# Moving small VectorE operations of a top-k attention and MLP kernel to other engines, converting weights earlier, and shifting attention towards the first sweep

## The chip, the cores and the metric

One core of one Trainium2 chip. The metric is the device time of one execution in microseconds (us). The engines are called as in the profile: PE (TensorE, with PEld for its weight loads), DVE (VectorE), ACT (ScalarE), POOL (GpSimd) and SP (SyncE, which here issues the DMAs).

## The reference, cut to what matters

```python
scores = scale * np.matmul(q, k.transpose(0, 1, 3, 2))      # 2 x 8 heads, 576 x 576, head size 64
kth = np.partition(scores, -32, axis=-1)[..., -32:-31]
scores = np.where(scores >= kth, scores, -1000000000.0)
attn = np.exp(scores - np.max(scores, axis=-1, keepdims=True))
attn = attn / (np.sum(attn, axis=-1, keepdims=True) + 1e-09)
x = np.matmul(attn, v)                                      # as 1152 tokens x 512

h = x @ w_in                                                # 512 -> 2048
sp = np.where(h > 20.0, h, np.log1p(np.exp(np.minimum(h, 20.0))))
y = (h * np.tanh(sp)) @ w_out                               # 2048 -> 512

out = ((y @ w_a) * (y @ w_b)) @ w_out2                      # 512 -> 1536 -> 512
```

The weights arrive as float64 (two 32-bit words each) and are turned into float32 on the chip.

## The kernel before, in words

The 1152 tokens are nine tiles of 128. **Attention** runs over steps, one for each tile and pair of heads, 36 in all. A step makes the scores on PE (`scores_`: `pq` L142, `psc` L174), copies them to `s2`, and then `largest` finds the 32 largest of each row on DVE in four rounds: for each head a MAX (L190), which gives the eight largest, and a MATCH_REPLACE (L193), which strikes them out, so 8 MAX and 6 MATCH_REPLACE a step. After the first round DVE makes the negated maxima `nm` (L195), and ACT takes the exponentials (L197). `weighted_sum_` masks and sums them on DVE (the masked sum, L211, twice a step), transposes them on PE (`pe`, L219) and multiplies by v (`px`, L226). Each round ends in a `yield`, so a step is four yields, and a tile of queries is ready 16 yields on. For the keys, `prep_k` splits k into a high and a low part (`km`, `kn`: cast on ACT, L114, subtraction at L115, on DVE for both batches).

The **MLPs** run over groups of tiles (`PLAN`): first tiles 0 and 1 together, then tile 2, then the second MLP for all three; then tiles 3 to 5 through both MLPs, then tiles 6 to 8. `gated` is the first MLP, 16 chunks of 128 hidden columns, each two weight blocks of 128 x 512. Its gate takes on ACT exp(h) (L387), on DVE the clamp to e^20 (L388), on ACT a square, a logarithm and an exponential (L389 to L391), and on DVE the gate's product (L392). `bilinear` is the second MLP, 12 chunks of three blocks. From tiles 0 to 2's second MLP on, the operands are split in two parts, and a product takes three matmuls.

I call the stretches of the program A (attention alone), G0 (the first MLP, tiles 0 and 1), G1 (tile 2), B0 (second MLP, tiles 0 to 2), G2 and B1 (tiles 3 to 5), and sweep three (tiles 6 to 8). A, G0, G1 and B0 are sweep one, G2 and B1 are sweep two.

The **weights** are converted once, by `convert_`, 68 blocks in the order of use: DMA of 512 KB into `w64` (three buffers), two ACT operations (L285, L286), a shift and mask on DVE (L287), then the exponent count is added on POOL (L290), and the sign comes in by one of two ways: ACT takes the sign (L289) and POOL multiplies by it (L291), or DVE ors the sign bit in (L293) and POOL adds (L294). `SIGN` says which blocks go which way: before, all 32 blocks of the first MLP go by ACT and POOL, and of the 36 of the second every fourth. The result is in `w` (11 buffers), is stored to DRAM as `ws`, and is also kept for its first use (`fresh`); later uses load it back as `raw` (five buffers, L315). How far ahead conversions run is set by `CONV`: its first number is how many are made in A, the second and third set how many are to be made by each chunk.

What runs beside what is set by `together`, which takes turns between attention and a group's chunks: `STEPS` says how many yields of attention go beside each group. The scheduler then sorts the instructions of each engine by priority, so an engine's order is fixed when the program is built, and each engine takes its queue in that order.

Of the kernel before, what the change touches and what calls it, by code (L numbers as in the profile page):

```python
# [9 lines left out]
F32 = mybir.dt.float32  # L10
# [3 lines left out]
AF = mybir.ActivationFunctionType  # L14
ALU = mybir.AluOpType
# [14 lines left out]

SUBS = (0, 0, 0, 0, 1, 1)

KSUB = 1

SIGN = (4, 1)

ABUF = (5, 3, 2, 1, 2, 3, 1, 2)
COPIES = (0, 0, 0, 1, 4, 2)

CONV = (5, 17, 13, 2)  # L40

STEPS = (24, 22, 18, 29, 28, 0, 5)

BUFS = (3, 11, 5, 6, 1)
NEG = -3.0e38
EXP20 = 485165195.40979


@with_exitstack
def topk_attention_mlps(ctx: ExitStack, tc: tile.TileContext, q, k, v, w, out):  # L50
# [6 lines left out]
    nc = tc.nc  # L57
# [46 lines left out]
    def prep_k(b, hp):  # L104
        ks = wp.tile([P, 2, J, D], F32, name="ks", bufs=BUFS[4])
        kr = wp.tile([R, 2, D], F32, name="kr", bufs=BUFS[4])
        for s in range(2):
            nc.sync.dma_start(ks[:, s], k[b, 2 * hp + s, 0:SM, :].rearrange("(p j) d -> p j d", j=J))
        nc.sync.dma_start(kr, k[b, 2 * hp:2 * hp + 2, SM:S, :].rearrange("h p d -> p h d"))
        km = wp.tile([P, 2, J, 2, D], F32R, name="km", bufs=BUFS[4])  # L110
        kn = wp.tile([R, 2, 2, D], F32R, name="kn", bufs=BUFS[4])
        for z, raw in ((km, ks), (kn, kr)):
            high, low = (z[..., i, :] for i in range(2))
            nc.scalar.copy(high, raw)  # L114
            (nc.gpsimd, nc.vector)[KSUB].tensor_sub(low, raw, high.bitcast(F32))  # L115
        for s in range(2):
            kk = kks[:, (b * H + 2 * hp + s) % (H + 2), :]
            pk = bank("pk")
            for j in range(J):
                nc.tensor.transpose(pk[:, j * P:(j + 1) * P], km[:, s, j].rearrange("p z d -> p (z d)").bitcast(F32),  # L120
                                    ident)
            pr = bank("pr", R)
            nc.tensor.transpose(pr, kn[:, s].rearrange("p z d -> p (z d)").bitcast(F32), ident[:R, :R])
            for src, o, n in ((pk, s * R, SM), (pr, SM * (1 - s), R)):
                nc.scalar.copy(kk[:, o:o + n], src)
            KK[b, 2 * hp + s] = kk
# [52 lines left out]
    def largest(s2):  # L179
# [6 lines left out]
        for r in range(TOPK // 8):  # L186
            got = slice(8 * r, 8 * r + 8)
            src = wk if r else s2
            for s in range(2):
                nc.vector.max(m8[:, s, got], src[:, s, :])  # L190
            if r < TOPK // 8 - 1:
                for s in range(2):
                    nc.vector.match_replace(wk[:, s, :], m8[:, s, got], src[:, s, :], NEG)  # L193
            if r == 0:
                nc.vector.tensor_scalar(nm, m8[:, :, 0], -1.0, None, op0=ALU.mult)  # L195
                for s in range(2):
                    nc.scalar.activation(e2[:, s, :], s2[:, s, :], AF.Exp, bias=nm[:, s:s + 1])  # L197
            yield
# [62 lines left out]

    order = [(z, f, i) for z, F in ((0, F1), (1, F2)) for f in range(F) for i in range(2 + z)]
    fresh, stored = {}, {}
    phase, made = [0], [0, 0, 0]

    def sub():

# [3 lines left out]
    def convert(n):  # L271
        with tc.high_priority(PRI[4]):
            convert_(n)

    def convert_(n):

        while len(stored) < min(n, len(order)):
# [14 lines left out]
            else:  # L292
                nc.vector.scalar_tensor_tensor(wi, high, -0x80000000, wi, op0=ALU.bitwise_and, op1=ALU.bitwise_or)  # L293
                nc.gpsimd.tensor_tensor(wi, wi, count, op=ALU.add)  # L294
            fresh[key] = wf
            stored[key] = dp.tile([P, U], F32, name=f"ws{len(stored)}")
            nc.sync.dma_start(stored[key], wf)

# [8 lines left out]

    def weight_(split, *key):

        convert(order.index(key) + 1)  # L310
        if key in fresh:
            raw = fresh.pop(key)
# [56 lines left out]
    def gated(block, tiles, yt, at, split, second):  # L369
# [10 lines left out]
        for f in range(F1):  # L380
# [3 lines left out]
            e = ep.tile([P, T], F32, name=f"e{T}")  # L384
            g = ep.tile([P, T], F32, name=f"m{T}")
            with tc.high_priority(PRI[2]):
                nc.scalar.activation(e, ph, AF.Exp)  # L387
                nc.vector.tensor_scalar(e, e, EXP20, None, op0=ALU.min)  # L388
                nc.scalar.activation(e, e, AF.Square, bias=1.0)  # L389
                nc.scalar.activation(e, e, AF.Ln, bias=half, scale=0.5)  # L390
                nc.scalar.activation(g, e, AF.Exp, scale=-1.0)  # L391
# [108 lines left out]
```

## Time and profile before

| | |
|---|---|
| median of 3 runs | 818.53 us (816.67 to 818.68) |
| the profiled execution | 815.02 us |
| its span, first to last instruction | 813.0 us |
| busy: PE / PEld | 686.1 us (84%) / 569.2 us (70%) |
| busy: DVE | 663.7 us (82%) |
| busy: ACT / POOL | 508.2 us (63%) / 433.8 us (53%) |
| DMA | 110.12 MB, 135 GB/s |

The shares are averages over stages with different limits. A window of the trace gives the busy time of each engine in a stretch; the groups give the mean time of one kind of instruction; the chain that ended last is followed back from the last instruction.

### The profile page before, as it was taken

Reading aid. Unit: us, or ns where it says so; the run is one execution under the profiler, and the core shown is the slowest. Engines: PE = TensorE matmul, PEld = TensorE weight load, DVE = VectorE, ACT = ScalarE, POOL = GpSimd, SP = SyncE. Lnnn points to the kernel's source line nnn. Section 1 sums busy time; section 2 is a strip of 40 time slices with the busy share of each in tenths; the row PEclk is TensorE's granted clock in tenths of the full one; section 3 lists DMA queues with packets and bytes.
Section 4 is the critical chain, followed back from the end, with each engine's and each line's share of the span. In section 5 each row is a group of like instructions: output and inputs, shape, how many; then the busy total and the mean of one; then the engine's idle time right before and its main releaser. Section 6 shows DMA issues by size and latency. Waiting matters only on the chain.

```text
span 813.0 us, 12328 instructions
## 1 busy us (share of the span) xinstructions
PE 686.1 (84%) x3988; PEld 569.2 (70%) x3988; DVE 663.7 (82%) x1335; ACT 508.2 (63%) x1135; POOL 433.8 (53%) x355
## 2 busy tenths in 40 slices
PE   4475657887648889899798899998999999989997
PEld 3354435555425667688687788887998989969996
DVE  4999999999996899999999899998984277743331
ACT  6874534888857987657667698885554355652222
POOL 4550001566657420069978766665655666665661
PEclk9966776989978999999999999999999999999999
DMA  8980100667857985216544443422233354443431
GB/s 250 325 240 10 27 1 1 167 209 194 219 159 246 343 253 157 56 63 182 166 127 135 119 128 91 120 88 65 81 105 91 96 164 130 130 117 86 135 105 39
DMA packets 70753, 110.12 MB, mean 135 GB/s; under 512 B 26529, under 2 KB 30625, under 8 KB 70689
## 3 DMA queue, kind: packets, MB, share of 16 engines
q1 hardware_dynamic: 70688, 109.34, 45.5%
q8 instruction: 31, 0.51, 0.2%
q14 instruction: 34, 0.27, 0.1%
HBM read 89.13 MB, written 20.19 MB: 134 GB/s over the span
## 4 chain that ended last, share of the span: by engine, by line
PE 40%; DVE 38%; ACT 7%; issue 6%; DMA 5%; POOL 3%; SPq 0%; ACTq 0%; DVEq 0%; POOLq 0%
PE ph L351 21%; DVE m L190 14%; DVE wk L193 11%; PE acc L358 7%; PE po L358 7%; DVE e L211 5%; DMA w<-in_w_dram 4%; DVE w L293 2%; PE px L226 2%; DVE w L287 2%; PE psc L174 1%; PE pe L219 1%; DVE e L388 1%; POOL w L291 1%; POOL w L290 1%
## 5 line engine op out<-in xcount | busy, mean ns | idle before, releaser
L325 POOL TENSOR_TENSOR whl<-raw,whl 128x512 fp32r<-128x512 f32 x128 | 168.2, 1320 | 96.1 <-ACT whl L324 58.3
L351 PE MATMUL ph<-yh,whl 128*128 128x384 f32 x576 | 160.8, 346 | 7.6 <-DVE m L416 5.6
L190 DVE MAX8 m<-wk 128x8 f32<-128x576 f32 x216 | 156.8, 747 | 0.4
L290 POOL TENSOR_TENSOR w<-w,w 128x512 int32<-128x512 int32 x41 | 55.1, 1345 | 141.1 <-DVE w L287 108.0
L351 PEld LDWEIGHTS ph<-yh,whl 128*128 128x128 f32 x576 | 107.1, 192 | 12.7 <-DVE m L416 7.2
L193 DVE MATCH_REPLACE8 wk<-m,wk 128x576 f32<-128x576 f32 x144 | 106.1, 739 | 0.0
L351 PE MATMUL ph<-yl,whl 128*128 128x384 f32 x288 | 99.1, 344 | 0.3 <-DVE yl L336 0.2
L226 PE MATMUL px<-et,v 128*64 128x128 f32 (+1 forms) x800 | 74.8, 298 | 7.9 <-ACT et L220 6.5
L219 PE MATMUL pe<-ident,e 128*128 128x128 f32 x324 | 55.3, 306 | 27.5 <-DVE e L211 21.6
L365 ACT CAST gh<-m 128x384 fp32r<-128x384 f32 x68 | 34.8, 512 | 68.2 <-DVE m L416 35.0
L325 POOL TENSOR_TENSOR whl<-w,whl 128x512 fp32r<-128x512 f32 x36 | 52.5, 1468 | 40.6 <-ACT whl L324 40.6
L366 POOL TENSOR_TENSOR gl<-m,gh 128x384 fp32r<-128x384 f32 x52 | 57.6, 1107 | 30.9 <-ACT gh L365 17.5
L226 PEld LDWEIGHTS px<-et,v 128*64 128x64 f32 x800 | 54.0, 152 | 28.4 <-ACT et L220 13.7
L351 PE MATMUL ph<-xh,whl 128*128 128x384 f32 x256 | 71.7, 340 | 0.6 <-DVE m L392 0.6
L211 DVE SCALAR_TENSOR_TENSOR e<-s,m,e 128x576 f32<-128x576 f32 x72 | 70.6, 987 | 1.1 <-ACT e L197 0.9
L219 PEld LDWEIGHTS pe<-ident,e 128*128 128x128 f32 x324 | 43.5, 157 | 35.1 <-issue 20.2
L220 ACT COPY et<-pe 128x384 f32<-128x384 f32 x108 | 49.8, 489 | 24.9 <-PE pe L219 24.1
L322 DVE CAST whl<-raw 128x512 fp32r<-128x512 f32 x59 | 42.4, 719 | 24.5 <-PE po L358 11.5
L324 ACT CAST whl<-raw 128x512 fp32r<-128x512 f32 x77 | 47.1, 621 | 24.1 <-PE ph L351 12.9
L197 ACT ACTIVATE e<-s,nm 128x576 f32<-128x576 f32 x72 | 52.3, 775 | 12.1 <-DVE nm L195 12.1
L358 PE MATMUL po<-whl,gh 128*128 128x512 f32 x216 | 58.9, 397 | 0.5 <-ACT gh L365 0.5
L174 PE MATMUL psc<-kks,qh 128*128 128x288 f32 x160 | 51.4, 342 | 9.2 <-ACT s L176 2.6
(87 smaller groups left out, 1619.9 us busy)
## 6 DMA issues: line engine op xcount, KB each, us to landing
raw<-ws SPq DMA_DIRECT2D x168, 256.0 KB, 2.7
w<-in_w_dram SPq DMA_DIRECT2D x68, 512.0 KB, 4.2
ws<-w SPq DMA_DIRECT2D x68, 256.0 KB, 4.3
qr<-in_q_dram SPq DMA_DIRECT2D x16, 256.0 KB, 4.1
ks<-in_k_dram SPq DMA_DIRECT2D x16, 128.0 KB, 4.5
v<-in_v_dram SPq DMA_DIRECT2D x16, 128.0 KB, 4.5
out_dram<-o SPq DMA_DIRECT2D x8, 256.0 KB, 2.8
qr<-in_q_dram SPq DMA_DIRECT2D x4, 128.0 KB, 4.8
```

Of the source, the lines that this page charges most:

```text
L174: nc.tensor.matmul(psc, qq[:, s, :], kk[:, a * HS:(a + 1) * HS], start=(n == 0), stop=(n == len(parts) - 1))
L190: nc.vector.max(m8[:, s, got], src[:, s, :])
L193: nc.vector.match_replace(wk[:, s, :], m8[:, s, got], src[:, s, :], NEG)
L197: nc.scalar.activation(e2[:, s, :], s2[:, s, :], AF.Exp, bias=nm[:, s:s + 1])
L211: nc.vector.scalar_tensor_tensor(e2[:, s, :], s2[:, s, :], kth[:, s:s + 1], e2[:, s, :], op0=ALU.is_ge, op1=ALU.mult, accum_out=sm[:, 2 * ...
L219: nc.tensor.transpose(pe[:, i, :], ef[:, n * P:(n + 1) * P], ident)
L226: nc.tensor.matmul(px[s * D:(s + 1) * D, o:o + n], vt[b][:, 2 * hp + s, j, :] if j < J else v4[b][:, hp, s, :], et[:, i if j < J else J, o ...
L290: nc.gpsimd.tensor_tensor(wi, wi, count, op=ALU.add)
L325: sub().tensor_sub(wl, raw, wh.bitcast(F32))
L351: nc.tensor.matmul(ph, a, x, start=(i == 0), stop=(i == len(mm) - 1))
L358: nc.tensor.matmul(acc[i], z[:, i * P:(i + 1) * P], a, start=(first and m == 0), stop=(last and m == len(mm) - 1))
L366: sub().tensor_sub(gl, g, gh.bitcast(F32))
```

## The change

```diff
-KSUB = 1
-
-SIGN = (4, 1)
+KSUB = (0, 1)
+
+SIGN = (4, 4)
...
-CONV = (5, 17, 13, 2)
-
-STEPS = (24, 22, 18, 29, 28, 0, 5)
+CONV = (26, 28, 15, 2)
+
+STEPS = (28, 25, 20, 26, 13, 0, 5)
...
-EXP20 = 485165195.40979
...
-            (nc.gpsimd, nc.vector)[KSUB].tensor_sub(low, raw, high.bitcast(F32))
+            (nc.gpsimd, nc.vector)[KSUB[b]].tensor_sub(low, raw, high.bitcast(F32))
...
-                nc.vector.tensor_scalar(nm, m8[:, :, 0], -1.0, None, op0=ALU.mult)
+                nc.scalar.mul(nm, m8[:, :, 0], -1.0)
...
-            fresh[key] = wf
+            if len(stored) < made[3] + BUFS[1] - 2:
+                fresh[key] = wf
...
+        made[3] = max(made[3], order.index(key))
         convert(order.index(key) + 1)
...
-                nc.scalar.activation(e, ph, AF.Exp)
-                nc.vector.tensor_scalar(e, e, EXP20, None, op0=ALU.min)
+                nc.vector.tensor_scalar(e, ph, 20.0, None, op0=ALU.min)
+                nc.scalar.activation(e, e, AF.Exp)
```

The key subtractions of batch 0 go to POOL. The negated maxima go to ACT. The signs of all 68 blocks go by ACT and POOL. The clamp is taken of h, by DVE from PSUM, before the exponential. A block that is converted nine or more places ahead of the block in use is not kept: it is stored, and loaded back when it is used (224 loads of `raw` in place of 168). 26 blocks are asked for in A. Attention's yields beside G0, G1 and B0 rise from 24, 22 and 18 to 28, 25 and 20.

The scheduler's order then holds these numbers of instructions in each stage, before and after. On DVE and ACT a stage begins with its first gate product (G) or bilinear product (B), on PE with its first product of the group. Line numbers are those of before.

| engine, instruction | A | G0 | G1 | B0 | G2 | B1 |
|---|---|---|---|---|---|---|
| DVE weight shift L287 | 12, 34 | 29, 34 | 8, 0 | 19, 0 | 0, 0 | 0, 0 |
| DVE sign L293 | 0, 0 | 6, 0 | 6, 0 | 15, 0 | 0, 0 | 0, 0 |
| DVE MAX L190 | 80, 82 | 48, 50 | 43, 50 | 44, 50 | 49, 48 | 24, 8 |
| DVE MATCH_REPLACE L193 | 60, 61 | 36, 39 | 32, 38 | 34, 36 | 36, 36 | 18, 6 |
| DVE masked sum L211 | 18, 20 | 12, 12 | 10, 12 | 13, 13 | 13, 13 | 6, 2 |
| DVE nm L195 | 10, 0 | 6, 0 | 6, 0 | 5, 0 | 6, 0 | 3, 0 |
| DVE key pairs L115 | 5, 1 | 0, 1 | 3, 2 | 0, 0 | 0, 0 | 0, 0 |
| PE psc L174 | 82, 82 | 46, 54 | 80, 80 | 40, 48 | 48, 48 | 24, 8 |
| PE pe L219 | 72, 72 | 45, 54 | 60, 63 | 45, 51 | 57, 51 | 45, 33 |
| PE px L226 | 80, 80 | 50, 60 | 90, 110 | 60, 50 | 70, 60 | 50, 40 |
| PE pq L142 | 22, 22 | 10, 12 | 12, 14 | 10, 10 | 14, 12 | 4, 2 |
| PE prs L240 | 16, 16 | 8, 8 | 8, 16 | 16, 8 | 8, 16 | 16, 8 |

Two places of DVE's order show what this does. The first is the middle of A. `m` is a step's list of largest scores, `s` the scores, `wk` the scores with the found ones struck out, `e` the exponentials, `ql` the low part of q. Before:

```order
L193 MATCH_REPLACE wk<-m_683,wk 128x576
L190 MAX m_760<-s_647 128x8
L193 MATCH_REPLACE wk<-m_683,wk 128x576
L193 MATCH_REPLACE wk<-m_760,s_647 128x576
L190 MAX m_683<-wk 128x8
L193 MATCH_REPLACE wk<-m_760,s_647 128x576
L195 TENSOR_SCALAR nm<-m_760 128x2
L190 MAX m_683<-wk 128x8
L153 SCALAR_TENSOR_TENSOR ql<-pq,qh 128x256
```

With the change (line numbers of the changed kernel):

```order
L189 MAX m_826<-wk 128x8
L192 MATCH_REPLACE wk<-m_936,s_768 128x576
L152 SCALAR_TENSOR_TENSOR ql<-pq,qh 128x256
L189 MAX m_826<-wk 128x8
L189 MAX m_936<-wk 128x8
L210 SCALAR_TENSOR_TENSOR e_824,sm<-s_646,m_826,e_824 128x576
L286 TENSOR_SCALAR w<-w 128x512
L189 MAX m_936<-wk 128x8
L210 SCALAR_TENSOR_TENSOR e_824,sm<-s_646,m_826,e_824 128x576
L192 MATCH_REPLACE wk<-m_936,wk 128x576 x2
L286 TENSOR_SCALAR w<-w 128x512
```

The search no longer has `nm` in it, and the weight shifts `w<-w` (now L286) stand between its pieces.

The second is the middle of B0; `m_...<-ph,e` is the bilinear product. Before:

```order
L287 TENSOR_SCALAR w<-w 128x512
L190 MAX m_4053<-wk 128x8 x2
L293 SCALAR_TENSOR_TENSOR w<-w_3897,w 128x512
L193 MATCH_REPLACE wk<-m_4053,wk 128x576
L287 TENSOR_SCALAR w<-w 128x512
L193 MATCH_REPLACE wk<-m_4053,wk 128x576
L190 MAX m_4053<-wk 128x8
L293 SCALAR_TENSOR_TENSOR w<-w_3910,w 128x512
L190 MAX m_4053<-wk 128x8
L211 SCALAR_TENSOR_TENSOR e_4051,sm<-s_3536,m_4053,e_4051 128x576
L153 SCALAR_TENSOR_TENSOR ql<-pq,qh 128x256
L416 TENSOR_TENSOR m_3709<-ph,e_3708 128x384
```

With the change:

```order
L192 MATCH_REPLACE wk<-m_4598,s_4226 128x576
L189 MAX m_4598<-wk 128x8
L192 MATCH_REPLACE wk<-m_4598,wk 128x576
L189 MAX m_4598<-wk 128x8
L189 MAX m_4598<-s_4226 128x8
L192 MATCH_REPLACE wk<-m_4598,wk 128x576
L192 MATCH_REPLACE wk<-m_4598,s_4226 128x576
L417 TENSOR_TENSOR m_4199<-ph,e_4198 128x384
L189 MAX m_4598<-wk 128x8 x2
L192 MATCH_REPLACE wk<-m_4598,wk 128x576
```

Shifts and signs are gone from this stage; between two bilinear products stands search alone.

## Rows read from the trace of the kernel before

**Rows 1.** Windows by stage: us, each engine's busy time, PE clock, DMA share, GB/s.

```profile
0.00:133.00 133.00, 76.52 (x408) 57.29 (x408) 121.90 (x269) 75.01 (x168) 31.58 (x30) 0.78 0.43 130
133.00:262.00 129.00, 94.03 (x426) 62.41 (x427) 121.62 (x244) 97.86 (x216) 78.79 (x64) 0.89 0.65 183
262.00:334.00 72.00, 63.48 (x485) 49.16 (x483) 67.15 (x162) 59.85 (x170) 17.50 (x24) 0.98 0.74 237
334.00:467.00 133.00, 118.26 (x763) 103.46 (x764) 131.31 (x246) 86.44 (x183) 100.00 (x74) 0.97 0.40 121
467.00:562.00 95.00, 91.27 (x569) 77.75 (x567) 90.77 (x191) 79.77 (x179) 60.74 (x49) 1.00 0.36 103
562.00:666.00 104.00, 103.23 (x641) 93.30 (x642) 64.40 (x121) 47.02 (x101) 63.44 (x52) 1.00 0.33 98
666.00:813.00 147.00, 139.29 (x702) 125.80 (x701) 66.55 (x107) 62.24 (x121) 81.80 (x65) 0.99 0.38 109
```

**Rows 2.** Chain that ended last, 562 to 666 us, by line.

```profile
by line: PE ph L351 54.2%; PE po L358 24.2%; PE px L226 7.8%; PE pe L219 5.3%; PE psc L174 2.8%; PE prs L240 1.6%; POOL gl L366 1.1%; issue 1.1%; PE pq L142 0.7%; DVE yl L336 0.6%; PE acc L358 0.5%; DVE whl L322 0.3%; POOL whl L325 0.2%
```

**Rows 3.** The same chain of the whole run, pieces: start, us, what.

```profile
60.04 2.65 DVE m L190 x4
75.65 1.48 DVE e L211 x4
79.84 1.46 DVE wk L193 x2
```

**Rows 4.** Groups of DVE, 0 to 133 us: busy us, mean ns | idle before.

```profile
L211 DVE SCALAR_TENSOR_TENSOR e<-s,m,e 128x576 f32<-128x576 f32 x16 | 12.6, 804 | 0.0
L287 DVE TENSOR_SCALAR w<-w 128x512 int32<-128x512 int32 x11 | 5.3, 482 | 2.1 <-ACT w L285 2.1
L115 DVE TENSOR_TENSOR km<-ks,km 128x512 fp32r<-128x512 f32 x5 | 4.5, 895 | 0.9 <-ACT km L114 0.9
L115 DVE TENSOR_TENSOR kn<-kr,kn 64x128 fp32r<-64x128 f32 x5 | 3.5, 691 | 0.3 <-ACT kn L114 0.3
L195 DVE TENSOR_SCALAR nm<-m 128x2 f32<-128x2 f32 x10 | 2.8, 284 | 0.0
```

**Rows 5.** Groups of DVE, 133 to 262 us.

```profile
L287 DVE TENSOR_SCALAR w<-w 128x512 int32<-128x512 int32 x30 | 17.7, 591 | 2.3 <-ACT w L285 2.3
L211 DVE SCALAR_TENSOR_TENSOR e<-s,m,e 128x576 f32<-128x576 f32 x14 | 15.6, 1125 | 0.0
L388 DVE TENSOR_SCALAR e<-e 128x256 f32<-128x256 f32 x16 | 12.0, 753 | 1.6 <-ACT e L387 1.6
L392 DVE SCALAR_TENSOR_TENSOR m<-m,ph 128x256 f32<-128x256 f32 x16 | 6.5, 406 | 1.7 <-ACT m L391 1.7
L293 DVE SCALAR_TENSOR_TENSOR w<-w,w 128x512 int32<-128x512 int32 x6 | 5.1, 842 | 0.1
```

**Rows 6.** Groups of DVE, 262 to 334 us.

```profile
L287 DVE TENSOR_SCALAR w<-w 128x512 int32<-128x512 int32 x8 | 4.6, 571 | 0.8 <-ACT w L285 0.7
L293 DVE SCALAR_TENSOR_TENSOR w<-w,w 128x512 int32<-128x512 int32 x6 | 4.1, 680 | 0.1
```

**Rows 7.** Groups of DVE, 334 to 467 us.

```profile
L293 DVE SCALAR_TENSOR_TENSOR w<-w,w 128x512 int32<-128x512 int32 x15 | 17.8, 1189 | 0.0
L287 DVE TENSOR_SCALAR w<-w 128x512 int32<-128x512 int32 x19 | 15.4, 811 | 0.0
```

**Rows 8.** Groups of POOL and ACT, whole run.

```profile
L291 POOL TENSOR_TENSOR w<-w,w 128x512 f32<-128x512 f32 x41 | 56.1, 1369 | 2.6
L289 ACT ACTIVATE w<-w 128x512 f32<-128x512 f32 x41 | 28.0, 682 | 0.1
```

**Rows 9.** Waits of the whole run: us in total, times, longest us.

```profile
PE acc L358 <- DVE m L392: 27.8, 14, 9.2
DVE w L287 <- ACT w L285: 5.2, 7, 1.3
```

**Rows 10.** Waits, 666 to 813 us.

```profile
ACT e L389 <- DVE e L388: 12.7, 13, 1.5
```

More of the change, by code (lines that the diff above doesn't have):

```diff
@@ L263, in topk_attention_mlps @@
     fresh, stored = {}, {}
-    phase, made = [0], [0, 0, 0]
+    phase, made = [0], [0, 0, 0, 0]
     def sub():
```

## The prediction

> **What bounds the kernel now.** I read the windows by stage first [rows 1]. They fall into two halves. From 0 to 467 us, the stages A, G0, G1 and B0, DVE is busy for 442 of 467 us, and in every one of the four it is busier than PE. From 467 us on, PE is busy for 91 of 95, 103 of 104 and 139 of 147 us. So sweep one lasts as long as DVE's queue, and what follows lasts as long as PE's work. The chain that ended last says the same of B1: 97% of it stands under PE's matmuls [rows 2]. A DVE saving therefore counts in sweep one, and a matmul moved out of sweeps two and three counts there. G2 alone is near both limits.
>
> Two readings give prices. The chain's pieces show the pace of a full DVE queue: four MAX in 2.65 us (0.66 each), two MATCH_REPLACE in 1.46 (0.73 each), two masked sums with their accumulator reads in 1.48 (0.74 each) [rows 3]. The groups, window by window, show that some DVE operations cost more the busier POOL is. POOL's share is 24% in A, 61% in G0 and 75% in B0 [rows 1]. The weight shift at L287 takes 482 ns in A, 591 in G0, 811 in B0 [rows 4, 5, 7], and the masked sum at L211 takes 804 in A and 1125 in G0 [rows 4, 5].
>
> **The change, stage by stage.** The counts are those of the table of the order; a stage's extra work on DVE is added to its length, since DVE sets it.
>
> *A.* Search and masked sums: two MAX, one MATCH_REPLACE and two sums more, 1.3 + 0.7 + 1.5 = +3.5 us. Shifts: 34 in place of the 11 of the window, at the 591 ns of G0, because POOL's share here comes near G0's (31.6 us, and 22 conversions with two operations of 1.37 [rows 8], and the key subtractions, some 98 us of about 149, or 66%): 20.1 - 5.3 = +14.8. For the same reason 20 masked sums at 1125 in place of 804 ns: +6.4. Gone from DVE: four pairs of key subtractions, 4 x (895 + 691) = -6.3, and the negated maxima, -2.8 [rows 4]. Sum **+15.6**. The ends: with 482 ns and no dearer sums it is +5.5; with 811 it is +23.1.
>
> *G0.* Search: two MAX and three MATCH_REPLACE, +3.5. Shifts: 34 for 30; POOL's share rises to about 79% (16 operations more), above B0's, but the neighbours are G0's, so I take 0.70, the middle of 591 and 811: 23.8 - 17.7 = +6.1. The six signs leave, -5.1, and seven negated maxima at A's 284 ns, -2.0. The clamp moves in front of the exponential, so its source is ph in PSUM. No row shows that form. The nearest is the gate's product at L392, also from PSUM, same shape, 406 ns, against 753 for the clamp as it stands [rows 5]: 16 x 0.347 = -5.6. One key pair of batch one comes here, +1.6. Sum **-1.5**; with 591 -5.2, with 811 +2.3.
>
> The clamp's row says that PSUM is the cheaper source here: 406 against 753 ns [rows 5]. The Trainium skill (VectorE: DVE Perf Modes, "Why PSUM operands drop a tier") says the reverse of it: an fp32 operation with one source runs at double rate from SBUF and at single rate from PSUM. By that rule alone the 16 clamps would not fall in price and the sum below would be some 6 us higher. The trace doesn't agree in this stage, since 753 ns for 256 columns is no double rate.
>
> *G1.* Seven MAX, six MATCH_REPLACE and two sums more, 4.6 + 4.4 + 1.5 = +10.5. Gone: eight shifts -4.6, six signs -4.1 [rows 6], one key pair -1.6. Sum **+0.2**.
>
> *B0.* No conversion is left: 19 shifts and 15 signs, -33.2 [rows 7]; six MAX and two MATCH_REPLACE come, +5.4. DVE alone would let the stage shrink by 27.8 of 133 us. But PE then becomes the bound. B1 has the same products and took 104 us at full PE [rows 1]. Against it, B0 has 24 score matmuls, six transposes of e and six of q more, and eight of the reciprocals' fewer. B1's shares over its counts price these at 0.121, 0.122, 0.18 and 0.104 us [rows 2]: +3.9, so 108. Some 8 us pass before the first product, hence 116: **-17**. The ends are -12, if PE doesn't keep that density, and -27.8, if PE gets the attention's part done earlier.
>
> *G2 and B1.* Two search steps have left for sweep one: 16 score matmuls, 18 transposes, 20 products with v and four transposes of q, at 0.121, 0.122, 0.162 and 0.18 us [rows 2]: 1.9 + 2.2 + 3.2 + 0.7 = **-8.0**, all on PE's path.
>
> *Sweep three.* The clamp before the exponential saves a handover between ACT and DVE. ACT waits there 12.7 us in 13 times for the clamp [rows 10], mostly behind PE; I take **-1**, between 0 and -12.7.
>
> At nothing I cost: the 27 signs and the negated maxima on ACT (0.68 us for a sign [rows 8]; with all three ACT operations of a conversion at that price, A's ACT goes from 75 to about 122 of 149 us, G0's from 98 to about 114, so both stay below DVE); the clamp's wait for ph, since PE waits 27.8 us for the gate and is ahead of DVE [rows 9], which if not so would cost DVE each lateness of PE; and 56 more reloads of 256 KB, 14 MB, in stages whose DMA share is 0.74 at most [rows 1], prefetched into five buffers. Shifts wait for ACT 5.2 us in all 68 [rows 9]; 23 more in A are worth 2 us and stand in the range.
>
> Sum: 15.6 - 1.5 + 0.2 - 17 - 8 - 1 = **-11.7 us**. The profiled execution took 815.0 us (span 813.0, 2.0 around it), so 803.3. The median of the runs is 818.5, 3.5 above it, and on that scale the forecast is 818.5 - 11.7 = 806.8, **807 us**. What a measurement of this kernel can tell from no change is about 0.3%, 2.5 us: 816 to 821 counts as the same.
>
> **The rivals.** *Better: sweep one keeps DVE's whole saving.* If the shifts in A stay at A's 482 ns and the sums at 804 (-10.1), or PE works off attention early enough in G1 that B0 shrinks by DVE's 27.8 (-10.8), the time is about 796, with both 786. For it: PE has idle time in G1 [rows 1]. Against it: POOL's share.
>
> *Slower: A and G0 are paced by POOL.* All 68 conversions are now packed into these two stages, with two POOL operations each. If POOL runs there nearly without gaps, each of the 68 shifts and 32 masked sums waits for a good part of a POOL operation. Half of one is 0.68 us [rows 8]; over the 482 and 804 of A that is 1.16 and 1.49 us, and against what I took: A 34 x 0.57 + 20 x 0.36 = 27, G0 34 x 0.46 + 12 x 0.36 = 20, together 47, or 854 us; a quarter of an operation gives about 820. It decides from 0.12 us a piece above my prices, since 100 x 0.12 is the whole gain. For it: the steps from 482 to 591 to 811. Against it: 811 at 75%, and the signs that leave DVE are such operations too. The Trainium skill (SBUF — State Buffer, "SBUF: two separate sides") states the rule behind it: POOL and those DVE operations hold one pair of ports exclusively, for a whole instruction. The rows agree in direction; they show 0.3 us at G0's share.
>
> *Nothing gained.* A at its upper end (+7.5), B0 at -12 (+5): 807 + 12.5 = 819. The freed time would lie idle on DVE in B0 and G2.
>
> **How the numbers follow.** My forecast, 798 to 816: 0.56. Better: 0.22. Nothing gained: 0.10. Slower: 0.12. The range takes in the better rival without its tail and reaches above to the quarter operation and the two waits of 2 us: 785 to 822. Faster: 0.22 + 0.51 of the 0.56 = 0.73; the same: 0.05 + 0.08 = 0.13; slower: 0.14.
>
> **What would show it.** Right: A longer by 10 to 20 us, G0 about as long, no L287 after G0, B0 near 116 us with PE over 95% busy and DVE idle there for the first time, B1 near 98. The clamp's mean at 256 columns near 406 ns. Wrong: shifts over 900 ns or masked sums over 1300 in A and G0 (POOL), B0 still full on DVE, or PE idle in B0 behind a reload or POOL's subtraction of the weight parts.

## The result, and the profile after

The changed kernel is slower, by a little: median 821.60 us of 8 runs (820.69 to 825.18) against 818.39 us of 8 runs of the kernel before (815.94 to 819.89). The ratio of the runs is 1.006, with a 95% interval of 1.0043 to 1.0076 (the two medians alone give 1.004). The forecast was 807 us, with a range of 785 to 822. The time lies just inside the range, but on the other side of no change. The profiled execution after took 821.38 us, its span 819.5 us, against 815.02 and 813.0 before. The spans thus differ by 6.5 us and the medians by 3.2, because the profiled execution before was 3.4 us faster than its median; what follows goes by spans.

DVE's busy time fell, as it was meant to: 663.7 us before, 620.4 us after. But the windows below show where the 43 us went: 36.8 of them left the last stretch, where PE sets the pace and DVE is idle for a third of the time and more, and 26.0 left B0, while A gained 7.8 and the middle 11.7. Over sweep one, which DVE bounded, its work fell by 6.5 us only. What has to be explained is why the middle got more work, and why that which left B0 and the last stretch gave so little.

For the comparison I cut both runs at the same three points of the program: the first product of G0, the first product of B0, and the first accumulation of G2. I call the second stretch, G0, G1 and the turn to B0, the **middle**. First the windows of the kernel before at these points (columns as in [rows 1]: length, then busy us of PE, PEld, DVE, ACT and POOL, PE's clock, DMA share, GB/s):

```profile
0.00:133.00 133.00, 76.52 (x408) 57.29 (x408) 121.90 (x269) 75.01 (x168) 31.58 (x30) 0.78 0.43 130
133.00:342.00 209.00, 162.30 (x969) 115.44 (x970) 196.77 (x425) 162.35 (x396) 96.29 (x87) 0.92 0.66 195
342.00:468.30 126.30, 114.77 (x712) 100.89 (x712) 123.31 (x227) 83.11 (x175) 101.30 (x75) 0.97 0.43 130
468.30:813.00 344.70, 332.48 (x1903) 295.55 (x1901) 221.72 (x416) 187.74 (x398) 204.67 (x164) 1.00 0.36 104
```

And after:

```profile
0.00:142.30 142.30, 80.00 (x409) 58.47 (x409) 129.65 (x269) 108.81 (x236) 89.70 (x76) 0.78 0.72 223
142.30:365.20 222.90, 177.97 (x1070) 126.61 (x1070) 208.51 (x447) 176.42 (x435) 114.90 (x100) 0.88 0.72 216
365.20:479.30 114.10, 111.77 (x689) 100.43 (x690) 97.30 (x195) 66.93 (x149) 63.15 (x51) 0.99 0.29 83
479.30:819.50 340.20, 328.67 (x1824) 290.64 (x1822) 184.91 (x355) 180.91 (x381) 205.93 (x164) 0.98 0.36 105
```

So A is 9.3 us longer, the middle 13.9 longer, B0 12.2 shorter, and the rest (G2 to the end) 4.5 shorter: +6.5 us in all. In B0, PE is busy for 111.8 of 114.1 us, and DVE, which had 3 us left there before, now has 17. In the middle DVE had 11.7 us more to do, although signs, negated maxima and part of the clamp had left it.

The groups of DVE say why. From 0 to 142 us (busy us, mean ns | idle before), which answers to [rows 4]:

```profile
L286 DVE TENSOR_SCALAR w<-w 128x512 int32<-128x512 int32 x30 | 17.6, 587 | 4.7 <-ACT w L284 4.7
L210 DVE SCALAR_TENSOR_TENSOR e<-s,m,e 128x576 f32<-128x576 f32 x16 | 17.3, 1092 | 0.0
```

From 142 to 282 us, which is G0 and answers to [rows 5]:

```profile
L286 DVE TENSOR_SCALAR w<-w 128x512 int32<-128x512 int32 x38 | 29.0, 764 | 2.4 <-ACT w L284 1.3 <-issue 0.8
L210 DVE SCALAR_TENSOR_TENSOR e<-s,m,e 128x576 f32<-128x576 f32 x16 | 18.4, 1159 | 0.0
L388 DVE TENSOR_SCALAR e<-ph 128x256 f32<-128x256 f32 x16 | 6.6, 411 | 1.9 <-PE ph L352 1.8
```

The shift costs 764 ns in G0, where 591 stood before. The clamp from PSUM costs 411 ns where 753 stood.

The middle ends with a turn. G1's last accumulation starts at 343.7 us, and B0's first product comes 21.5 us later; before, these were 331.2 and 342.0, 10.8 us apart. All lengths of the turn below are counted so. PE's timeline in the turn, before and after (start, us, engine, line, op, [idle before and its releaser]):

```profile
330.74 1.02 PE L358 MATMUL acc<-raw,m 128*128 128x512 f32 x2
...
339.21 0.60 PE L341 MATMUL pt<-ident,y 128*128 128x128 f32 x4
339.65 0.60 PE L219 MATMUL pe<-ident,e 128*128 128x128 f32 x4
341.83 0.44 PE L219 MATMUL pe<-ident,e 128*128 128x128 f32 x2 [1.58 <-DVE e L211]
342.02 0.72 PE L351 MATMUL ph<-yh,whl 128*128 128x384 f32 x2
```

After:

```profile
343.31 1.02 PE L359 MATMUL acc<-raw,m 128*128 128x512 f32 x2
...
348.30 1.09 PE L239 MATMUL prs<-ident,rs 128*64 128x128 f32 x16 [0.89 <-DVE rs L235]
...
353.92 0.85 PE L173 MATMUL psc<-kks,ql 128*128 128x288 f32 x2 [3.03 <-DVE ql L152]
...
359.56 2.15 PE L218 MATMUL pe<-ident,e 128*128 128x128 f32 x9 [3.84 <-DVE e L210]
361.64 1.11 PE L225 MATMUL px<-et,v 128*64 128x128 f32 x6
362.69 0.66 PE L342 MATMUL pt<-ident,y 128*128 128x128 f32 x4
...
365.18 0.62 PE L352 MATMUL ph<-yh,whl 128*128 128x384 f32 x2 [0.45 <-ACT yh L335]
```

B0's first product needs y of tile 2 transposed (`pt`). In PE's fixed queue `pt` now stands behind `pe`, the transposes of an attention step's `e`, which wait for that step's search on DVE; before, it stood in front of them. The chain of 344 to 365 us agrees: nearly all of it is search.

```profile
by line: DVE m L189 47.9%; DVE wk L192 38.8%; DVE e L210 7.0%; issue 5.3%; DVE x L241 2.8%; DVE ql L152 1.6%; DVE rs L234 0.3%; DVE rs L235 0.3%
```

DVE works through the whole turn (21.0 of the 21 us from 344 to 365). The turn is therefore not a stall of DVE; it is DVE's backlog of attention, made visible on PE.

Counted over the same four stretches, MAX and MATCH_REPLACE together are: before 132, 155, 92 and 126, after 131, 181, 95 and 98. The 28 that left the last stretch did not go to B0, where DVE now idles. They went to the middle, where DVE is busy for 208.5 of 222.9 us.

### The profile page after: what moved, and what is told of

Same layout as the page of the kernel before. It is cut to its first block, busy times and chain, and to the rows that moved or that the text cites. A ratio compares the mean times of both kernels' runs of the same rounds, so it can differ in the third digit from the quotient of the medians.

```text
span 819.5 us, 12468 instructions
## 1 busy us (share of the span) xinstructions
PE 698.4 (85%) x3988; PEld 576.2 (70%) x3988; DVE 620.4 (76%) x1264; ACT 533.1 (65%) x1198; POOL 473.7 (58%) x390
## 4 chain that ended last, share of the span: by engine, by line
PE 55%; DVE 8%; ACT 1%; issue 1%; POOL 0%; DMA 0%; ACTq 0%; POOLq 0%
PE ph L352 28%; PE po L359 9%; PE acc L359 8%; DVE m L189 4%; PE px L225 3%; DVE wk L192 3%; PE pe L218 2%; PE psc L173 2%; DVE e L210 1%; PE pq L141 1%; PE pt L342 1%; PE prs L239 1%; ACT y L400 1%; DVE m L393 0%; DMA raw<-ws 0%
## 5 line engine op out<-in xcount | busy, mean ns | idle before, releaser
L326 POOL TENSOR_TENSOR whl<-raw,whl 128x512 fp32r<-128x512 f32 x161 | 214.0, 1337 | 166.7 <-ACT whl L325 136.8
L352 PE MATMUL ph<-yh,whl 128*128 128x384 f32 x576 | 157.8, 345 | 1.5 <-ACT yh L335 1.5
L289 POOL TENSOR_TENSOR w<-w,w 128x512 int32<-128x512 int32 x68 | 89.3, 1313 | 73.0 <-DVE w L286 38.7
L325 ACT CAST whl<-raw 128x512 fp32r<-128x512 f32 x110 | 67.6, 622 | 45.5 <-PE ph L352 22.0
L290 POOL TENSOR_TENSOR w<-w,w 128x512 f32<-128x512 f32 x68 | 94.0, 1383 | 5.4 <-ACT w L288 0.7
L417 DVE TENSOR_TENSOR m<-ph,e 128x384 f32<-128x384 f32 x36 | 20.0, 555 | 88.1 <-PE ph L352 80.1
L218 PE MATMUL pe<-ident,e 128*128 128x128 f32 x324 | 56.9, 313 | 29.5 <-DVE e L210 20.1
L210 DVE SCALAR_TENSOR_TENSOR e<-s,m,e 128x576 f32<-128x576 f32 x72 | 74.8, 1048 | 1.8 <-ACT e L196 1.2
L284 ACT ACTIVATE w<-w 128x512 f32<-128x512 f32 x68 | 45.9, 675 | 31.3 <-DMA w<-in_w_dram 19.4
L189 DVE MAX8 m<-s 128x8 f32<-128x576 f32 x72 | 53.2, 748 | 15.7 <-ACT s L175 15.5
L173 PE MATMUL psc<-kks,ql 128*128 128x288 f32 x160 | 49.2, 339 | 17.6 <-DVE ql L152 17.6
```

Of the source, the lines that this page charges most:

```text
L173: nc.tensor.matmul(psc, qq[:, s, :], kk[:, a * HS:(a + 1) * HS], start=(n == 0), stop=(n == len(parts) - 1))
L210: nc.vector.scalar_tensor_tensor(e2[:, s, :], s2[:, s, :], kth[:, s:s + 1], e2[:, s, :], op0=ALU.is_ge, op1=ALU.mult, accum_out=sm[:, 2 * ...
L218: nc.tensor.transpose(pe[:, i, :], ef[:, n * P:(n + 1) * P], ident)
L290: nc.gpsimd.tensor_mul(wf, wf, highf)
L325: nc.scalar.copy(wh, raw)
L326: sub().tensor_sub(wl, raw, wh.bitcast(F32))
```

## The experiments

The change has three separable parts. I call them the **moves** (key subtractions of batch 0 and all signs off DVE, negated maxima to ACT, clamp ahead of the exponential), the **early conversions** (`CONV` and the rule for kept blocks) and the **shares** (`STEPS`). Lengths below are given for A, middle, B0, rest; those of the kernel before are 133.0, 209.0, 126.3 and 344.7 us. Times are medians, and each ratio is against the kernel before on the same chip.

### The parts alone and in pairs

**e1_engines**: the kernel before with the moves alone.

```diff
+KSUB = (0, 1)
+SIGN = (4, 4)
...
+                nc.scalar.mul(nm, m8[:, :, 0], -1.0)
...
+                nc.vector.tensor_scalar(e, ph, 20.0, None, op0=ALU.min)
+                nc.scalar.activation(e, e, AF.Exp)
```

> Before, with the four moves between engines only (key subtractions of batch 0 and all signs on POOL, negated maxima on ACT, clamp ahead of the exponential); conversions and attention's shares as before. Theory 1 (the early conversions lose the time, by making shifts dearer in A and G0 and by leaving DVE idle in B0; the moves by themselves gain): 795 to 808 us. Theory 2 (the moves lose it, because 37 us more of POOL's work blocks DVE): 819 to 830 us.

Measured 817.90 us, 1.0021 (1.0002 to 1.0039): no gain. Its windows:

```profile
0.00:129.30 129.30, 76.19 (x409) 57.26 (x409) 116.18 (x250) 76.43 (x178) 37.56 (x38) 0.80 0.45 134
129.30:339.10 209.80, 166.82 (x963) 116.86 (x963) 181.37 (x397) 172.06 (x418) 113.38 (x99) 0.92 0.65 194
339.10:475.90 136.80, 127.25 (x844) 110.39 (x845) 134.98 (x270) 105.71 (x232) 122.10 (x91) 0.98 0.42 124
475.90:816.20 340.30, 322.87 (x1775) 286.08 (x1774) 183.89 (x350) 178.73 (x371) 205.76 (x163) 0.99 0.36 103
```

In the middle DVE is busy for 181.4 us, 15.4 less than before, and the stretch is no shorter: the freed time became idle time, 28.4 us where there were 12.2. What DVE waited for in the middle (us in total, times, longest), in the kernel before:

```profile
DVE m L392 <- ACT m L391: 4.2, 5, 2.1
DVE w L287 <- ACT w L285: 3.1, 4, 1.2
```

and in e1:

```profile
DVE m L392 <- ACT m L391: 11.9, 7, 3.1
DVE w L287 <- ACT w L285: 8.2, 9, 2.5
DVE e L387 <- PE ph L351: 4.3, 6, 1.7
```

These are handovers of the gate (its product `m` waits for ACT, the clamp `e` for PE's `ph`) and of the weights (the shift waits for ACT). The order put 34 more search operations into B0 (126 for 92), where conversions still stand, so B0 grew by 10.5. Neither theory held.

**g1_convonly**: the kernel before with the early conversions alone.

```diff
-CONV = (5, 17, 13, 2)
+CONV = (26, 28, 15, 2)
...
+            if len(stored) < made[3] + BUFS[1] - 2:
```

> Before, with the early conversions and their rule only: old shares, old engines. If the early conversions gain by themselves (B0 bound by PE, some 100 us): 808 to 815 us. If they gain only beside the moves that make room on DVE in A and G0: 820 to 835 us (the kernel with the new shares too, 841, less the 10 to 13 us that the shares cost).

Measured 827.59 us, 1.0113 (1.0088 to 1.0139). A 151.8, middle 213.0, B0 113.5, rest 348.5. B0 falls by 12.8, but A pays 18.8, with DVE busy for 140 of its 152 us.

**e4_engines_conv**: moves and early conversions, that is, the changed kernel with the old shares.

```diff
-STEPS = (28, 25, 20, 26, 13, 0, 5)
+STEPS = (24, 22, 18, 29, 28, 0, 5)
```

> The changed kernel with attention's shares as before (the moves, the early conversions and the rule stay). Theory 1: 816 to 826 us, A and G0 still long. Theory 3 (the new shares of attention lose the time, by the wait between G1 and B0 that grew from 11 to 21 us): 805 to 812 us, and that wait back at 11 us.

Measured 811.09 us, 0.9934 (0.991 to 0.9958). Each of the two alone gains nothing or loses; together they gain. A takes 151.8 us in g1 and 142.0 here, so the conversions need the room that the moves make on DVE there; B0 takes 136.8 us in e1 and 112.5 here, so the moves need it free of conversions.

```profile
0.00:142.00 142.00, 80.14 (x409) 58.63 (x409) 127.36 (x269) 108.40 (x236) 89.43 (x76) 0.75 0.72 223
142.00:351.50 209.50, 171.66 (x970) 119.07 (x970) 184.37 (x407) 168.20 (x415) 112.14 (x99) 0.89 0.74 226
351.50:464.00 112.50, 112.49 (x744) 101.05 (x745) 101.77 (x204) 69.57 (x154) 66.22 (x53) 1.00 0.34 94
464.00:809.00 345.00, 331.87 (x1869) 294.75 (x1867) 200.47 (x386) 186.08 (x394) 205.08 (x163) 0.99 0.36 102
```

The middle is as long as before (209.5), although DVE has 12.4 us less to do there; no engine is full in it. DVE's waits for the gate are again the largest:

```profile
DVE m L394 <- ACT m L393: 8.3, 7, 1.8
DVE e L389 <- PE ph L353: 6.4, 8, 2.1
```

B0 is already at PE's limit (112.49 busy of 112.50) without the new shares.

**e2_schedule** (early conversions and shares, no moves), **e3_engines_steps** (moves and shares) and **h2_steps_only** (shares alone, on the kernel before) complete the set. All three have this line, e2 also g1's edit and e3 also e1's:

```diff
-STEPS = (24, 22, 18, 29, 28, 0, 5)
+STEPS = (28, 25, 20, 26, 13, 0, 5)
```

> Before, with the early conversions, the rule on what is kept and the new shares of attention only; all operations on their old engines. Theory 1: 822 to 840 us, since the 27 signs on DVE now also stand in A and G0. Theory 2: 805 to 818 us.

> The changed kernel with the conversions and the rule on what is kept as before (the moves and the new shares of attention stay). Theory 1: 795 to 808 us, shifts spread over A, G0, G1 and B0 as before. Theory 2: 819 us or more, as the changed kernel.

> Before, with the new shares of attention only. If the shares lose whatever the rest is: 826 to 832 us (10 to 13 more, as in the two pairs measured). If they lose only because of the place of the transposes, which here stand behind two thirds of a step: 818 to 825 us.

Measured: e2 840.84 us, 1.029 (1.0257 to 1.0322); e3 831.13 us, 1.0176 (1.0145 to 1.0207); h2 827.13 us, 1.0126 (1.0108 to 1.0145). The shares lose wherever they are added. By spans and stretches:

| shares added to | A | middle | B0 | rest | span |
|---|---|---|---|---|---|
| the kernel before (h2) | +1.5 | +9.2 | +0.7 | +0.2 | +11.6 |
| the moves (e1 to e3) | +1.7 | +11.7 | +2.9 | -4.3 | +12.0 |
| moves and early conversions (e4 to after) | +0.3 | +13.4 | +1.6 | -4.8 | +10.5 |

The loss is in the middle each time. What DVE did in the middle, in us:

| kernel | length | DVE busy | DVE idle |
|---|---|---|---|
| before | 209.0 | 196.8 | 12.2 |
| shares alone (h2) | 218.2 | 212.9 | 5.3 |
| moves (e1) | 209.8 | 181.4 | 28.4 |
| moves and shares (e3) | 221.5 | 199.6 | 21.9 |
| moves and early conversions (e4) | 209.5 | 184.4 | 25.1 |
| all three (after) | 222.9 | 208.5 | 14.4 |

The moves take work from DVE and give it back as idle time. The shares bring 16 to 24 us of work and lengthen the stretch by 9 to 13, since a part of it fills idle time.

### Is it the place of one step, or the amount of attention in the middle?

My first reading of the turn was that one attention step stands in front of `pt`, and that taking it out would restore the 10.8 us. **f2_g1_22** takes three yields out of G1, **f5_mid** takes G0 and G1 back to the old shares and gives B0 more; both are the changed kernel but for `STEPS`.

```diff
-STEPS = (28, 25, 20, 26, 13, 0, 5)
+STEPS = (28, 22, 23, 26, 13, 0, 5)
```

> The changed kernel with three of attention's yields moved from G1 to B0 (28, 22, 23, 26, 13): in PE's order the transposes of tile 2's y then stand in front of the transposes of one more attention step, where the changed kernel has them behind. Theory 3 (the time is lost in the wait between G1 and B0, because those transposes stand behind a step that DVE has yet to search): the wait falls from 21 to 10 to 12 us, the time to 808 to 813. Theory 1 (the early conversions lose it in A and G0, the wait only takes up what is late anyhow): 818 us or more.

Measured 814.92 us, 0.9979 (0.9953 to 1.0004). The turn is 17.6 us, not the 10 to 12 expected, and the middle 220.2: a miss. `pt` does stand a step earlier, but 174 search operations are still ahead of B0's first product. The time is 7 us below the changed kernel's, in small parts: middle and B0 some 3 us each, the rest 2.

```diff
-STEPS = (28, 25, 20, 26, 13, 0, 5)
+STEPS = (24, 22, 24, 27, 15, 0, 5)
```

> The changed kernel with attention's yields 24, 22, 24, 27, 15: A, G0 and G1 as with the old shares, and six yields more in B0, where DVE stood idle 15 of 113 us. Theory 3: the wait stays near 10 us, and the work comes out of sweep two: 804 to 810 us, at or below the kernel with the old shares (811). If B0 has no room: 812 or more.

Measured 811.12 us, 0.9929 (0.991 to 0.9949). The middle is 212.9 with 160 search operations. But more yields for B0 put no more search there (101; e4 had 103), so it gains nothing over e4. Its profiled execution took 816.03 us, the longest of its eight, so its stretches are some 5 us long in sum against the median.

**h1_same_sum** gives G0 and G1 together the 46 yields that they had before, and B0 the rest, so that sweep one has the changed kernel's 73.

```diff
-STEPS = (28, 25, 20, 26, 13, 0, 5)
+STEPS = (28, 18, 27, 26, 13, 0, 5)
```

> The changed kernel with attention's yields 28, 18, 27, 26, 13: sweep one has 73 yields as in the changed kernel, but seven of them stand behind the end of G1, so that in PE's order the transposes of tile 2's y follow the last product of G1 at once. If the loss is in those transposes' place (theory 3): the wait between G1 and B0 falls from 21 us below 8, and the time to 803 to 810 us. If sweep one merely has too much attention in it, and the wait is where that shows: 814 us or more, with the time given back in G1 or B0.

Measured 814.10 us, 0.997 (0.9955 to 0.9984). `pt` comes right behind G1's last accumulation and the turn falls to 5.3 us, as expected. The time falls by 7.5 us against the changed kernel, not by the 12 to 19 expected, since G0 and G1 take back 6 of the 16 us (207.5 for 201.4) and the rest is 3.5 us longer. This lies on the border of the two readings and does not part them: the edit moves `pt` and takes nine search operations out of the middle at once. The turn by itself is not the measure, since 16 us of it are worth 10 in the middle; the middle as a whole, 212.8 us with 172 search operations, is the thing to look at.

Over all kernels here but two, the middle goes with that count: with 154 to 160 search operations it takes 203 to 213 us (before, e1, e4, f5, and f8, g2, g5, h4 below), with 163 to 172 it takes 213 (g1, h1, and g4 below), with 174 to 181 it takes 218 to 223 (f2, h2, e3, after, and f4 below). The exceptions are g3, 219.5 us with 159, and e2, 232.0 us with 180, which has 27 signs on DVE in the middle besides. From e4 to after it is 23 operations and two masked sums for 13.4 us; at 0.735 us and 1.1 us a piece they are 19 of the 24.1 us by which DVE's work grew, and DVE's idle time fell by 10.7. The count and the place of `pt` change together in most of these kernels, so that the count is the cause is argued from DVE's work, not shown by an edit that changes it alone.

### What POOL's work costs DVE

**f4_nomul**: the changed kernel without POOL's multiplication by the sign.

```diff
-                nc.gpsimd.tensor_mul(wf, wf, highf)
```

> The changed kernel without POOL's multiplication by the sign (weights keep no sign): 68 operations, 94 us, less on POOL in A and G0. Theory 4 (POOL's work makes DVE's shifts and masked sums dearer there): shifts fall from 587 and 764 ns to below 520 in both stages, masked sums from 1092 and 1159 to below 1000, A and G0 together from 282 to 262 to 270 us. If DVE's prices have another cause: prices as they are, 278 us or more.

Measured 808.04 us, 0.9892 (0.987 to 0.9914). POOL's busy time in the middle falls from 114.9 to 57.2 us. DVE's groups from 142.9 to 282 us:

```profile
L286 DVE TENSOR_SCALAR w<-w 128x512 int32<-128x512 int32 x33 | 16.1, 489 | 3.0 <-ACT w L284 2.3 <-issue 0.6
L210 DVE SCALAR_TENSOR_TENSOR e<-s,m,e 128x576 f32<-128x576 f32 x16 | 15.6, 984 | 0.0
L387 DVE TENSOR_SCALAR e<-ph 128x256 f32<-128x256 f32 x16 | 6.6, 414 | 7.9 <-PE ph L351 7.9
```

The shift goes from 764 to 489 ns in G0 and from 587 to 413 in A, the masked sum from 1159 to 984 in G0 but only from 1092 to 1044 in A (below 1000 was expected), with nothing taken out but POOL's multiplication. The clamp, whose source is now in PSUM, does not move (411 and 414). A and G0 together end at 274 us (ACT's first copy of G0's y, at 281 in the changed kernel), between the two expectations. The time falls by 13.6 us (11.9 in the profiled executions), but not all of it by these prices: in the middle DVE has 15.9 us less to do and the stretch is 5.2 us shorter, A is 0.6 longer, and 7.3 us come from B0 and the rest, where nothing is converted. The Trainium skill (SBUF — State Buffer, "SBUF: two separate sides") has the rule that a POOL operation and a DVE operation in a two-port mode or with two inputs in SBUF hold a shared pair of ports exclusively, for the whole instruction; this run agrees with it for the shift and the sum.

**f8_signdve**: e4 with the second MLP's signs back on DVE (and the old shares).

```diff
-SIGN = (4, 4)
+SIGN = (4, 1)
```

> The changed kernel with the old shares of attention, and the signs of 27 blocks back on DVE: against the kernel with the old shares (811 us) it shows what the move of the signs is worth where conversions are early. The move pays (DVE is full there): 820 to 832 us. It doesn't, since POOL's multiplications cost DVE as much in dearer shifts: 807 to 815 us.

Measured 809.71 us, 0.9912 (0.9885 to 0.994), against e4's 811.09 and 0.9934: the move of the signs is worth nothing. In the middle 27 signs come to 20.1 us on DVE, the 38 shifts fall from 25.6 to 20.2 us because POOL has 77 in place of 112 us to do, and most of the rest goes into the 25 us in which DVE idled in e4's middle, of which 18 are left.

### The other moves, each taken back from f8

**g2_noclamp** puts the clamp behind the exponential again, **g3_nonm** the negated maxima on DVE, **g4_noksub** all key subtractions on DVE.

```diff
-                nc.vector.tensor_scalar(e, ph, 20.0, None, op0=ALU.min)
-                nc.scalar.activation(e, e, AF.Exp)
+                nc.scalar.activation(e, ph, AF.Exp)
+                nc.vector.tensor_scalar(e, e, 485165195.40979, None, op0=ALU.min)
```

> Early conversions, old shares, 27 signs on DVE (810 us), and the clamp back behind the exponential. By the rows the clamp's move saves DVE some 7 us in G0 and G1: 813 to 819 us. By the rule on PSUM sources alone it saves nothing: 807 to 812 us.

Measured 813.62 us, 0.9949 (0.9929 to 0.9968): the clamp's move is worth about 4 us, at the lower end of what was expected. Its old form cost 506 ns here, with POOL busy for 44% of G0, against 753 at 61% in [rows 1, 5].

```diff
-                nc.scalar.mul(nm, m8[:, :, 0], -1.0)
+                nc.vector.tensor_scalar(nm, m8[:, :, 0], -1.0, None, op0=ALU.mult)
```

> The same base (810 us) with the negated maxima back on DVE. By the rows they cost DVE some 6 us in A, G0 and G1: 814 to 818 us. If ACT's round trip hides them: 807 to 812 us.

Measured 826.66 us, 1.011 (1.0079 to 1.014), 17 us over f8 and far over what I expected (some 9 us above the upper end). `nm` itself is busy for 9.0 us in A and the middle, which are 5.5 and 9.7 us longer. The remaining 6 us there, and the middle that is long for its count of searches, I cannot put down to `nm`; the order changed with it. That stays open.

```diff
-KSUB = (0, 1)
+KSUB = (1, 1)
```

> Early conversions, old shares, 27 signs on DVE (810 us), and the key subtractions of batch 0 back on DVE. By the rows the move saves DVE 5 to 6 us in A: 813 to 817 us. If POOL's later subtractions cost PE and DVE as much: 807 to 811 us.

Measured 818.54 us, 1.0032 (1.001 to 1.0054), some 9 us over f8 and above what I expected. A is 4.8 us longer, the middle 3.3 and B0 4.5, the rest 5.6 shorter in the profiled execution, which at 815.3 us was faster than the median.

### A version that beats both

**g5_best** joins f5's shares with f8's signs, **h4_sum_signdve** h1's shares with f8's signs. h4 against the changed kernel:

```diff
-SIGN = (4, 4)
+SIGN = (4, 1)
...
-STEPS = (28, 25, 20, 26, 13, 0, 5)
+STEPS = (28, 18, 27, 26, 13, 0, 5)
```

> The same base (810 us) with attention's yields 24, 22, 24, 27, 15. The version meant to be the fastest: 803 to 809 us if six more yields beside B0 fill DVE's idle time there and leave sweep two; 809 to 812 if, as with the signs on POOL, the scheduler leaves B0's order as it was.

> The yields 28, 18, 27, 26, 13 and 27 signs back on DVE, all else as changed. Meant to beat both kernels: 802 to 809 us if the transposes' place was the loss and the signs on DVE cost nothing; 810 us or more if not.

Measured: g5 810.16 us, 0.9894 (0.9865 to 0.9924), no better than f8. h4 **801.36 us, 0.9816 (0.9793 to 0.984)**, the fastest here. Its windows:

```profile
0.00:143.10 143.10, 80.47 (x409) 59.12 (x409) 127.43 (x269) 109.09 (x237) 89.68 (x76) 0.77 0.72 222
143.10:346.40 203.30, 169.04 (x972) 118.61 (x972) 197.29 (x431) 155.39 (x389) 79.22 (x72) 0.91 0.73 238
346.40:462.10 115.70, 114.32 (x754) 101.80 (x752) 104.17 (x216) 69.33 (x157) 66.58 (x53) 1.00 0.30 87
462.10:798.40 336.30, 326.31 (x1860) 291.41 (x1857) 198.30 (x378) 182.56 (x391) 204.28 (x162) 0.99 0.36 103
```

Its search counts are 131, 156, 108 and 111: one more than before in the middle, 16 more in B0, 15 fewer in the last stretch. This is what the shares were thought to do. h1, with the same yields, had 172 and 92 in the middle and B0; the scheduler's order put 16 operations elsewhere once the signs were DVE's. So taking the signs back is worth 12.7 us here and nothing in f8. For the 9.5 us of it in the middle the order is the likely reason, not the signs' own price: DVE does 4.8 us less there and idles 4.7 us less. That isn't shown by an edit of the order alone. With equal search left in the last stretch, h4 is 8.4 us shorter there than the kernel before and h1 only 1.0. PE's idle time makes 4.5 of the 7.4 us between them, and its busy time 2.9. Part of both lies where G2 hands over to B1. In h1, PE waits there 4.2 us for ACT's copy of y, and then has a granted clock of 0.52, close to the lower of its two levels (1.2 GHz), for 14 us; in h4 the same place shows 0.83 over 10 us. First h1, then h4:

```profile
561.00:575.00 14.00, 9.45 (x34) 7.83 (x35) 13.26 (x29) 6.21 (x12) 0.00 (x0) 0.52 0.06 19
550.00:560.00 10.00, 7.40 (x40) 5.92 (x39) 10.00 (x21) 7.70 (x17) 2.53 (x2) 0.83 0.14 46
```

Why h1's handover takes longer I have not settled.

## Why the prediction was wrong

Against its own terms, by the three cuts:

| stretch | forecast | measured |
|---|---|---|
| A, G0, G1, up to B0's first product | +15.6 - 1.5 + 0.2 = +14.3 | +9.3 + 13.9 = +23.2 |
| B0 | -17 | -12.2 |
| G2, B1, sweep three | -8 - 1 = -9 | -4.5 |
| sum | -11.7 | +6.5 |

That the time lies inside the range is luck of opposite errors: -6.3 us in A against +15.2 in the middle, +4.8 in B0 and +4.5 behind it. By part of the change, with the prediction's own terms (the split is mine: B0's -17 counts with the conversions) and the spans:

| part | forecast | measured |
|---|---|---|
| moves and early conversions (before to e4) | -17.7 | -4.0 |
| of that, up to B0's first product, behind A | -1.3 - 14.0 = -15.3 | +0.5 |
| shares (e4 to after) | 14.0 - 8.0 = +6.0 | +10.5 |

**The step that failed is the rule "a stage's extra work on DVE is added to its length, since DVE sets it", where it credits savings to G0 and G1.** Without the search and sums that arrive there (3.5 + 10.5 = 14.0 us), the prediction has these two stages shrink by 15.3 us, for the signs, the negated maxima and the clamp, less dearer shifts. The saving itself was nearly right: e4 has 12.4 us less work on DVE in the middle. But the stretch is 0.5 us longer. In e1 it is 15.4 us less work and 0.8 us longer. The whole saving became DVE's idle time, 25.1 and 28.4 us where the kernel before has 12.2. DVE was the busiest engine there but no longer the pace: it waits at the gate's handovers. The clamp's wait for `ph`, which the prediction put at nothing "since PE waits 27.8 us for the gate and is ahead of DVE", is 6.4 us in e4, 4.3 in e1 and 3.5 after; the gate product's wait for ACT is 4.2 us before and 8.3 and 11.9 in e4 and e1. That these waits are what holds the stretch up is read from the traces; no run takes them away.

**The shares were mis-sized too**, by 4.5 us. The prediction added by stage and never set their price beside their return; by its own terms they lose 6 us, and the three pairs of runs show 10.5 to 12.0. The arrival looks right (14.0 forecast, 9.2 to 13.4 measured in the middle), but by luck: DVE's work there grew by 16.1 to 24.1 us, and idle time took up the rest. The return was 0 to 5 us in place of 8. Some of it may have gone to the clock: in the last stretch the granted clock is 1.00 before and 0.98 after, which for a full PE is at most some 7 us (an estimate: 2% of 340 us). And B0 could pay nothing back, since with the conversions gone it stands at PE's limit whether the shares are old or new (112.5 and 114.1 us).

**The counts hid a part of it.** The table of the order gave G0 and G1 18 search operations more and B0 8. In the trace the middle has 26 more and B0 3, so search costs DVE some 6 us more in the middle than was summed. The order's stage on an engine ends where that engine reaches the next stage's instruction, and in the turn DVE's search runs on for 21 us while PE waits for it. The prediction kept "some 8 us before the first product" from [rows 1] as a constant; it measured 18.7 on that scale, the 10.7 by which the turn grew being added. G0, forecast "about as long", takes 140 us for 129. G1's sum also leaves out its own negated maxima and clamps, savings that would have put the forecast further off.

**POOL's price in G0 was too low.** I took 700 ns for the shift, "the middle of 591 and 811". It is 764, and four shifts slid from A into G0. In the middle the shifts cost 6.7 us more than before, where 1.5 stood in the sum. f4 shows that POOL's work is what makes them dear. The rival "A and G0 are paced by POOL" had this mechanism but put it at 13 us and more above my prices; shifts stayed under the 900 ns and sums under the 1300 that were to show it. Against the sum's own prices it was worth a few us. A itself came out cheaper than forecast, 9.3 against 15.6: 31 shifts and 16 sums fall into it where I counted 34 and 20.

**B0 was bound by PE, as said.** DVE idles there for the first time and PE is 98% busy. The estimate of 108 us for PE's work in it was low by some 4: the stretch has 111.8 us of it.

**Right:** the clamp from PSUM, 406 ns by the nearest row, 411 measured. The prediction weighed a rule against it from the Trainium skill (VectorE: DVE Perf Modes, "Why PSUM operands drop a tier"), by which fp32 from PSUM goes at single rate. It set that aside because "753 ns for 256 columns is no double rate", and there it read a mean of two kinds of calls. Before, six of G0's 16 clamps from SBUF took 269 to 278 ns and ten 835 to 1386; after, all 16 from PSUM took 401 to 425. The quick calls agree with the rule. The move paid because it ended the slow ones, which waited for POOL. The signs' removal from the middle (9.2 us forecast, 9.1 gone) and that of the negated maxima from A (2.8) were sized right on DVE. But f8 shows that the signs gave it all back through POOL's load on the shifts and through DVE's idle time.

The rival nearest in time was "nothing gained", 819 us: freed time idle on DVE in B0, and B0 at -12. That is what B0 did. It placed the idle time in B0 and G2 and not in the middle, and it lacked the search there, which turned no gain into a loss.

## What to carry to other kernels

Work taken off the busiest engine shortens a stretch only as long as that engine does not wait at handovers: set its idle time and what ends it beside the saving, and expect the saving to reappear there. Set a forecast up by part of the change as well as by stage: a share of work moved from one stage to another has a price where it arrives and a return where it leaves, and a stage that another part has just brought to a different engine's limit pays no return. A handover between stages lasts as long as the backlog that stands in front of it in an in-order queue, so count the moved work up to the first product of the next stage and not up to the engine's own stage mark. Two parts that each gain nothing may gain together, when one frees the room that the other needs.

## What the hardware showed that I had not expected

The mean price of the same DVE operation rises with POOL's load when its operands lie in SBUF, and not when the source is PSUM. The shift in G0 cost 489, 546, 591 and 764 ns with POOL busy for 34, 43, 61 and 74% of the stretch (f4, f8, before, after). The clamp of 128 x 256 cost 506 and 753 ns from SBUF (44 and 61%, g2 and before), but 414, 411 and 411 from PSUM (34, 43 and 74%, f4, f8, after). The search operations, also in SBUF, stayed at 0.74 to 0.75 us on average in all of these. The shares of POOL are its busy time over the length of G0 (129 us before, a window of 140 in the others).

These means mix two prices, which the timeline of the kernel before shows. A clamp that starts well inside one of POOL's operations ends just after that operation; one that starts between two of them, or as one ends, takes 0.27 us:

```profile
170.76 1.30 POOL L290 TENSOR_TENSOR w<-w,w 128x512 int32<-128x512 int32 x1 [0.52 <-DVE w L287]
171.33 0.88 DVE L388 TENSOR_SCALAR e<-e 128x256 f32<-128x256 f32 x1
190.36 1.30 POOL L290 TENSOR_TENSOR w<-w,w 128x512 int32<-128x512 int32 x1 [0.46 <-DVE w L287]
191.60 0.27 DVE L388 TENSOR_SCALAR e<-e 128x256 f32<-128x256 f32 x1
```

All ten slow clamps of G0 before end 145 to 153 ns after the end of a POOL operation. All 26 of the 68 shifts before that took over 450 ns end 280 to 289 ns after one; the others took some 410. So a busier POOL does not make each operation dearer: it makes more of them wait for its operation to end (9 of 30 shifts in G0 before, 17 of 38 after, 3 of 33 in f4).
